# Two layers of multi-query and Hedgehog attention: slab prefetch in the weight fold, and where VectorE closes the query features

## The chip, the cores and the metric

The kernel runs on one core of a Trainium2 chip. The core has TensorE (PE in the profile; PEld are its weight loads), VectorE (DVE), ScalarE (ACT), GpSimd (POOL) and SyncE (SP, which issues most DMAs). Each engine works through its own queue in order and waits on semaphores for the others. The metric is the device time of one execution in microseconds; lower is better.

## The reference

The input is x of 2048 tokens by 576 features in fp32. Four residual blocks follow one another: A, B, A, B, the same weights each time.

```python
# A: softmax attention, 32 query heads of 18, one shared key and value head
q = (x @ wq) per head;  k = x @ wk;  v = x @ wv
o = softmax(q k^T * 18**-0.5) @ v;  return o @ wo
# B: Hedgehog linear attention, 32 heads of 18
q, k, v = x @ wqkv per head
phi_q = concat(softmax(q @ w_phi), softmax(-(q @ w_phi)));  phi_k likewise
kv = phi_k^T v;  z = sum_s phi_k
return (phi_q kv) / (phi_q z + 1e-6) @ wo
x = x + A(layernorm(x)); x = x + B(layernorm(x)); and both once more
```

## The kernel before

**Layers and stages.** One "layer" of the kernel is a block A and a block B. Each layer has an attention stage (softmax attention over 16 token tiles of 128, in two groups of 16 heads each, so 32 groups) and a tail that reads out the linear attention and projects the next layer's queries. The attention stage is the bulk of the time: in the profile 112 to about 1240 us for the first layer and 1478 to about 2565 us for the second.

**A group.** For each of 16 key tiles `expose` (L990) multiplies scores into a two-bank PSUM tile (`sc`, L518; three such tiles exist) and ScalarE takes their exponential (L994). `add_values` (L804) multiplies the exponentials with the values (L806) into one PSUM bank. `burst` puts three such score tiles ("units") on TensorE, then two or three steps of values.

**Two PSUM banks for everything else.** `homes` holds two banks, called `ps` and `acc`. One collects the current group's values. The other is the spare in which all background work is done, one product at a time. When a group opens (`values`, t = 0) the two change places: the spare becomes the new group's bank, so whatever product stands in it must have been copied out by VectorE before the first value product of the group can start, and the old bank is the spare once `finish_group` has transposed it out (L908, into `turned`).

**Background work.** The generator `stream` runs beside the groups. In the first layer it first folds w_phi into the query and key weights (`fold_phi`, ten slabs of 128 rows, loaded by ScalarE's DMA queue, L332). Then it runs `output` for finished tiles (the projection with `wo`, L240 with `on`, and the residual add, L304) and `mix` for 14 of the 16 tiles. A `mix` makes, in this order: two key products, two value products, two query products (14 matmuls each, L240), and the state products (`update_state`, L595) which VectorE adds to `kv` (L601).

**Features.** After each key or query product `feature_start` copies the bank out (L551), takes maxima and minima (L553, L554) and subtracts them (L555, L556); ScalarE takes the exponential (L558). `feature_end`, the "closing", sums, inverts and multiplies (L563, L564, L565). For the queries, whose tile is `featq`, both halves are closed at the end of `mix`. Then VectorE transposes 32x32 blocks of the whole query features into `pht` (L647, in `block_transpose`), and four DMAs spill that to DRAM (L652, `phi<-pht`). The rest of this generator is put into the queue `slow`.

**The next tile's tokens.** `turn_tokens`, called from `update_state` right behind the state sum, splits the next tile's transposed tokens into two parts (`xs`, lines 133, 134, 673, 674). The tokens were transposed earlier by `flip` (L658, L647 on `xc`, also through `pht`), through DRAM; `flip` is called only while `slow` is empty.

**What sets the order.** `tick` takes one step from each of the queues `urgent`, `loads` and `slow`. `in_order` pins TensorE's and VectorE's instructions in the order in which the Python code makes them. ScalarE's, GpSimd's and SyncE's instructions are placed by the framework's scheduler, by readiness as it estimates it.

## Time and profile before

| | us |
|---|---|
| median of 3 runs | 2717.02 (2711.14 to 2718.07) |
| profiled execution | 2717.63 |
| its span, first to last instruction | 2715.9 |
| TensorE busy | 2609.6 (96%) |
| ScalarE busy | 2149.7 (79%) |
| VectorE busy | 1258.2 (46%) |
| mean granted TensorE clock | 0.986 |

The profile is of one execution; times in it count from its first instruction. In a row of the timeline stand the start, the duration, the engine, the line of the kernel, the operation, the output and inputs by tile names, their sizes, and in brackets how long the engine stood idle before it and who ended that. A row of waits gives the total, how often, and the longest. Value products of one step run four at a time on different columns of the array, so that durations of single rows overlap.

### The profile page before, as it was taken

To read this page: it belongs to the slowest core of one execution; us is meant where nothing else is said; L and a number is where in the kernel's file an instruction comes from. 1 tells how busy PE (TensorE), PEld (TensorE's weight loads), DVE (VectorE), ACT (ScalarE), POOL (GpSimd) and SP (SyncE) were. 2 spreads that over 40 slices of the span, in tenths; PEclk is the share of its full clock that TensorE was granted. 3 is DMA by queue.
4 is the path that set the end of the run, shared out by engine and by line. 5 is a ranking of instruction groups with operands and counts; after the bars stand their busy time and mean duration, and the time that the engine had idled before them with its cause. 6 is when DMAs were issued, how large, how long until landed. Compare 5 with 4: busy or idle time off the path is not lost. (4 is left out here: it accounts for less than half of the span.)

```text
span 2715.9 us, 55458 instructions
## 1 busy us (share of the span) xinstructions
PE 2609.6 (96%) x22030; PEld 1454.6 (54%) x22030; DVE 1258.2 (46%) x2867; ACT 2149.7 (79%) x2511; POOL 56.8 (2%) x98
## 2 busy tenths in 40 slices
PE   7989999999999999999998999999999999999989
PEld 6633345554555544456997244444444444444588
DVE  8532244445454444445775124444444444444455
ACT  4588898998889879995334999999999999999711
POOL 1000000000000000001000000000000000000010
PEclk9999999999999999999999999999999999999989
DMA  6554134222223212214755412222222222221164
GB/s 192 169 186 140 50 111 130 69 66 58 53 67 72 59 46 57 57 47 112 233 155 161 144 51 59 59 59 59 59 59 59 59 59 59 57 59 48 40 190 144
DMA packets 476349, 245.05 MB, mean 90 GB/s; under 512 B 222706, under 2 KB 433842, under 8 KB 476082
## 3 DMA queue, kind: packets, MB, share of 16 engines
q1 hardware_dynamic: 474610, 238.46, 31.8%
q8 instruction: 177, 2.90, 0.5%
q10 hardware_dynamic: 1472, 2.95, 0.3%
q14 instruction: 90, 0.74, 0.1%
HBM read 133.86 MB, written 105.51 MB: 88 GB/s over the span
## 5 line engine op out<-in xcount | busy, mean ns | idle before, releaser
L994 ACT ACTIVATE pt<-sc 128x1024 f32<-128x1024 f32 x2036 | 1925.4, 1047 | 211.2 <-PE sc L518 191.1
L518 PE MATMUL sc<-qst,kst 56*128 56x512 f32 x3840 | 687.1, 449 | 23.5 <-ACT pt L994 23.0
L518 PEld LDWEIGHTS sc<-qst,kst 56*128 56x128 f32 x3840 | 317.2, 184 | 534.3 <-ACT pt L994 479.4
L806 PE MATMUL acc<-pt,vst 128*32 128x512 f32 x4096 | 499.0, 600 | 0.6 <-DVE featk L551 0.2
L806 PE MATMUL ps<-pt,vst 128*32 128x512 f32 x4048 | 483.5, 601 | 6.5 <-DVE featk L551 6.1
L806 PEld LDWEIGHTS ps<-pt,vst 128*32 128x32 f32 x4048 | 110.1, 109 | 237.4 <-issue 224.2
L806 PEld LDWEIGHTS acc<-pt,vst 128*32 128x32 f32 x4096 | 106.0, 109 | 218.4 <-issue 212.1
L240 PE MATMUL ps<-wahi,xs 128*128 128x288 f32 x792 | 174.5, 306 | 5.7 <-DVE featk L551 3.4
L304 DVE TENSOR_TENSOR xc<-xc,acc 128x288 f32<-128x288 f32 x60 | 27.2, 453 | 321.1 <-PE acc L240 321.1
L240 PEld LDWEIGHTS ps<-wahi,xs 128*128 128x128 f32 x792 | 131.6, 191 | 14.1 <-DVE featk L551 4.2
L240 PE MATMUL ps<-walo,xs 128*128 128x288 f32 x440 | 130.1, 298 | 0.0
L240 PE MATMUL acc<-wdhi,on 128*128 128x288 f32 x540 | 119.7, 307 | 2.0 <-DMA on<-od 2.0
L240 PE MATMUL ps<-wchi,xs 128*128 128x288 f32 x495 | 111.2, 310 | 0.0
L131 ACT ACTIVATE xs<-ps 128x512 fp32r<-128x512 f32 x36 | 21.4, 595 | 112.6 <-PE ps L290 106.3
L396 PE MATMUL ps<-xsc,wbhi 128*128 128x256 f32 x576 | 107.6, 286 | 0.7 <-ACT xsc L131 0.7
L551 DVE COPY featq<-ps 128x288 f32<-128x288 f32 x47 | 21.5, 458 | 179.7 <-PE ps L240 179.6
L418 ACT ACTIVATE pc<-ps 128x256 fp32r<-128x256 f32 x80 | 30.4, 384 | 93.4 <-PE ps L396 90.4
L240 PEld LDWEIGHTS acc<-wdhi,on 128*128 128x128 f32 x540 | 87.9, 187 | 23.9 <-issue 21.1
L396 PEld LDWEIGHTS ps<-xsc,wbhi 128*128 128x128 f32 x576 | 91.4, 193 | 1.6 <-ACT xsc L131 1.1
L240 PEld LDWEIGHTS ps<-wchi,xs 128*128 128x128 f32 x495 | 82.8, 192 | 16.8 <-issue 15.6
L240 PE MATMUL acc<-wdlo,on 128*128 128x288 f32 x300 | 88.2, 294 | 0.0
L396 PE MATMUL ps<-xsc,wblo 128*128 128x256 f32 x320 | 86.1, 284 | 0.0
(260 smaller groups left out, 3066.6 us busy)
## 6 DMA issues: line engine op xcount, KB each, us to landing
qst<-qd SPq DMA_DIRECT2D x360, 72.0 KB
od<-parts SPq DMA_DIRECT2D x512, 36.0 KB
pht<-phi SPq DMA_DIRECT2D x32, 540.0 KB
qd<-pc SPq DMA_DIRECT2D x64, 256.0 KB
phi<-pht SPq DMA_DIRECT2D x112, 144.0 KB
on<-od SPq DMA_DIRECT2D x60, 256.0 KB
xd<-xc SPq DMA_DIRECT2D x32, 288.0 KB
flipped<-pht SPq DMA_DIRECT2D x112, 72.0 KB
```

The source lines that it names most:

```text
L131: A.activation(dst_hi, src, AF.Copy)
L240: T.matmul(dst, xs[:, slot, :], w[half][:, k, c0 : c0 + HALF], start=(n == 0), stop=(n == last))
L304: V.tensor_add(xr, xr, po)
L396: T.matmul(po, lhs, xsc[:, slot, :], start=(n == 0), stop=(n == LASTP))
L418: A.activation(pc[:, 0, :], po, AF.Copy)
L518: T.matmul(sc, kst[head_rows(h), t * P : (t + 1) * P], q[head_rows(h), h // 2, :], start=True, stop=True)
L551: V.tensor_copy(e[:, hs, 0, :], src)
L806: T.matmul(acc[32 * j : 32 * j + 32, :], vst[:, t, :], pts[j], start=first, stop=last)
L994: A.activation(pt, sc, AF.Exp, scale=SCALE)
```

## The change

Three edits. First, `fold_phi` loads three slabs before its loop, and in the loop asks for slab n + 3 at the end of turn n instead of for slab n + 2 at its start. Second, the closing of the first half of the query features moves from the end of `mix` to the end of `queries`, ahead of the state products; the second half stays where it was. Third, the transposition into `pht` is no longer made at the end of `mix` but in the first step that `tick` takes of the generator in `slow`; the four spills follow four ticks later as before, counted from there.

```diff
-        st, following = fetch(0), fetch(1)
+        slabs_in = deque(fetch(n) for n in range(3))
...
-        short(pl, st)
+        short(pl, slabs_in[0])
         yield -110
         for n, (half, k) in enumerate(units):
-            later = fetch(n + 2)
+            st = slabs_in.popleft()
...
-            short(pl, following)
+            short(pl, slabs_in[0])
+            slabs_in.append(fetch(n + 3))
             nc.sync.dma_start(scratch[half, k * P : (k + 1) * P, :], fo[:, :D])
-            st, following = following, later
...
         if copies is A:
             for b in range(2):
                 feature_end(e, b, G)
+        else:
+            feature_end(e, 0, V)
...
         yield from update_state(ek, vb, st, ps, after=after)
-        for b in range(2):
-            feature_end(eq, b, V)
-        blocks = bw.tile([P, NKG, P], F32, name="pht").rearrange("p a b -> p (a b)")
-        spilling = block_transpose(blocks[:, : 2 * D], eq.rearrange("p h s d -> p (h s d)"), spill[i], SPILL)
-        next(spilling)
-        slow.append(spilling)
+        feature_end(eq, 1, V)
+
+        def spilling():
+            blocks = bw.tile([P, NKG, P], F32, name="pht").rearrange("p a b -> p (a b)")
+            yield from block_transpose(blocks[:, : 2 * D], eq.rearrange("p h s d -> p (h s d)"), spill[i], SPILL)
+
+        slow.append(spilling())
```

The changed kernel's line numbers are 2 higher from L613 on and 3 higher behind `mix`: L647 is L649 there, L908 is L911, L994 is L997.

TensorE's rows are in the same order in both kernels through both attention stages. On VectorE, around the state sum of the first layer's tenth mixer tile (the one at 965 us in the profile), before:

```order
L555 TENSOR_TENSOR featq<-fmin,featq 128x16x18
L556 TENSOR_TENSOR featq<-featq,fmax 128x16x18
L908 STREAM_TRANSPOSE turned<-acc 128x512
L601 TENSOR_TENSOR kv<-kv,ps 128x288
L133 CAST xs<-xn 128x512
```

And with the change:

```order
L556 TENSOR_TENSOR featq<-featq,fmax 128x16x18
L563 TENSOR_REDUCE fz<-featq 128x32
L564 RECIPROCAL fz<-fz 128x32
L565 TENSOR_TENSOR featq<-featq,fz 128x576
L911 STREAM_TRANSPOSE turned<-acc 128x512
L601 TENSOR_TENSOR kv<-kv,ps 128x288
L133 CAST xs<-xn 128x512
```

The three instructions of the first closing stand ahead of the closed group's transposition, the state sum and the token split. A few rows on, the same queue and tile, before:

```order
L134 TENSOR_TENSOR parts<-osb,parts 128x512
L563 TENSOR_REDUCE fz<-featq 128x32
L564 RECIPROCAL fz<-fz 128x32
L565 TENSOR_TENSOR featq<-featq,fz 128x576
L563 TENSOR_REDUCE fz<-featq 128x32
L564 RECIPROCAL fz<-fz 128x32
L565 TENSOR_TENSOR featq<-featq,fz 128x576
L647 STREAM_TRANSPOSE pht<-featq 128x1152
L551 COPY featk<-ps 128x16x18
```

And with the change:

```order
L134 TENSOR_TENSOR parts<-osb,parts 128x512
L563 TENSOR_REDUCE fz<-featq 128x32
L564 RECIPROCAL fz<-fz 128x32
L565 TENSOR_TENSOR featq<-featq,fz 128x576
L551 COPY featk<-ps 128x16x18
L553 TENSOR_REDUCE fmax<-featk 128x16
L554 TENSOR_REDUCE fmin<-featk 128x16
L555 TENSOR_TENSOR featk<-fmin,featk 128x16x18
L556 TENSOR_TENSOR featk<-featk,fmax 128x16x18
L649 STREAM_TRANSPOSE pht<-featq 128x1152
```

One closing is left ahead of the next tile's copy, and the transposition stands behind that copy and its four followers. It does so at seven of the 28 tiles, six of them in the first layer; at the others the transposition stays ahead of the next copy.

On ScalarE, from the query exponentials of the sixth tile (737 us) to the seventh's, before:

```order
L558 ACTIVATE featq<-featq 128x576
L994 ACTIVATE pt<-sc 128x1024 x9
L558 ACTIVATE featk<-featk 128x576
L994 ACTIVATE pt<-sc 128x1024 x2
L558 ACTIVATE featk<-featk 128x576
L994 ACTIVATE pt<-sc 128x1024 x31
```

And with the change:

```order
L558 ACTIVATE featq<-featq 128x576
L997 ACTIVATE pt<-sc 128x1024 x6
L558 ACTIVATE featk<-featk 128x576
L997 ACTIVATE pt<-sc 128x1024 x6
L558 ACTIVATE featk<-featk 128x576
L997 ACTIVATE pt<-sc 128x1024 x30
```

The next tile's first key exponential stands three score tiles further ahead, behind six of them instead of nine. The same holds for the tile at 799 us.

On SyncE, from the first tile's spills (453 us), before `L652 DMA phi x4`, the next group's query loads (L502, L509), then the flipped tokens (L652); with the change three of the spills, the query loads, the fourth spill, then the flipped tokens.

## The prediction

> **What bounds the kernel now.** I read the page's busy times first, then the busy times by stage, then TensorE's own waits in each stage, and last the timeline around its longest stops.

> ```profile
> span 2715.9 us, 55458 instructions
> PE 2609.6 (96%) x22030; PEld 1454.6 (54%) x22030; DVE 1258.2 (46%) x2867; ACT 2149.7 (79%) x2511; POOL 56.8 (2%) x98
> 400.00:1200.00 800.00, 781.84 (x6574) 401.12 (x6574) 385.83 (x780) 711.12 (x771) 7.03 (x13) 1.00 0.27 67
> 1500.00:2500.00 1000.00, 990.14 (x8028) 469.84 (x8024) 409.94 (x824) 925.28 (x1001) 7.56 (x14) 1.00 0.25 62
> ```

> The last two rows are the two attention stages with the mixer's tiles in them (columns: length, then busy PE, PEld, DVE, ACT, POOL, then clock, DMA share, GB/s). TensorE is busy for 781.84 of 800 us in the first layer and 990.14 of 1000 in the second. All that a reordering of VectorE can win there is TensorE's idle time: 18 us and 10 us. Its waits, the first five rows from the first layer (400 to 1200), the last from the second (1500 to 2500), say for whom (total, times, longest):

> ```profile
> PE ps L806 <- DVE featk L551: 6.1, 1, 6.1
> PE sc L518 <- ACT pt L994: 4.3, 11, 1.2
> PE ps L240 <- DVE featk L551: 3.4, 2, 1.7
> PE ps L240 <- DVE turned L908: 1.3, 3, 0.5
> PE acc L240 <- DMA on<-od: 0.6, 1, 0.6
> PE sc L518 <- ACT pt L994: 9.3, 28, 0.7
> ```

> In the second layer nothing but the exponentials is waited for; VectorE holds up nobody, so I look for no gain there. In the first layer one stop of 6.1 us and two of 1.7 end with L551, the copy that empties a PSUM bank. These three are what the change can reach.

> **The first edit (slabs).** The order shows ScalarE's queue beginning with three slab loads in both kernels, and the later ones at the same rows; TensorE's and VectorE's rows are unchanged up to the first mixer tile. The prefetch was already there, so this edit is worth nothing; if the order hid a difference it would touch only the fold stage before 400 us.

> **The second and third edits, at the long stop.** The closing (L563, L564, L565) of the query features' first half now stands ahead of `turned` (L908) and the state sum; L647 stands behind the copy.

> ```profile
> 962.22 2.78 PE L806 MATMUL acc<-pt,vst 128*32 128x512 f32 x24
> 969.03 0.97 PE L518 MATMUL sc<-qst,kst 56*128 56x512 f32 x6
> 976.09 5.05 PE L806 MATMUL ps<-pt,vst 128*32 128x512 f32 x24 [6.09 <-DVE featk L551]
> 965.07 0.72 DVE L908 STREAM_TRANSPOSE turned<-acc 128x512 f32<-128x512 f32 x1 [1.45 <-PE acc L806]
> 970.51 0.75 DVE L563 TENSOR_REDUCE fz<-featq 128x32 f32<-128x576 f32 x1
> 972.36 0.74 DVE L563 TENSOR_REDUCE fz<-featq 128x32 f32<-128x576 f32 x1
> 974.32 1.38 DVE L647 STREAM_TRANSPOSE pht<-featq 128x1152 f32<-128x1152 f32 x1
> 975.62 0.42 DVE L551 COPY featk<-ps 128x288 f32<-128x288 f32 x1
> ```

> One closing takes 972.36 - 970.51 = 1.85 us, or 974.32 - 972.36 = 1.96 to the next instruction; L647 delays the copy by 975.62 - 974.32 = 1.30. The closing put ahead of L908 finds 1.45 us of idle time there, so L908 and all behind it, TensorE's next product too, come 1.85 - 1.45 = 0.40 late. The second closing starts at 970.91, the copy at 970.91 + 1.96 = 972.87, and TensorE goes on 0.47 later, as now (975.62 to 976.09): 973.34 instead of 976.09, **2.75 us won**. TensorE then stands idle from 969.03 + 0.97 + 0.40 = 970.40 for 2.94 us.

> The stop has a second price: 24 value products took 5.05 us behind it, and 2.78 at 962. The clock explains the 2.27 us between (columns as above; the clock is the third number from the end):

> ```profile
> 975.00:980.00 5.00, 3.91 (x20) 0.99 (x24) 2.77 (x6) 0.68 (x1) 0.00 (x0) 0.50 0.56 138
> 301.04 0.30 PE L337 MATMUL ps<-idf,fstage 128*72 128x128 f32 x1 [1.80 <-DVE featk L362]
> 301.00:303.00 2.00, 1.96 (x9) 0.27 (x9) 0.29 (x1) 0.35 (x1) 0.00 (x0) 0.61 0.34 82
> 303.00:305.00 2.00, 2.00 (x13) 1.24 (x10) 0.00 (x0) 1.09 (x2) 0.00 (x0) 0.53 0.59 190
> ```

> An idle time of 1.80 us at 301 was enough for a halved clock: (0.39 + 0.47) x 2 / 0.5 = 3.4 us of it, which cost 1.7. So I take it that 2.94 us idle still halves the clock, for 1.7 us of loss: 2.27 - 1.70 = **0.57 won**. The ends are 0 and 2.27. Rival D below is the other case.

> [...]

> **The two stops of 1.7 us** (tiles at 737 and 799, alike):

> ```profile
> 737.00 0.46 DVE L601 TENSOR_TENSOR kv<-kv,ps 128x288 f32<-128x288 f32 x1 [1.98 <-PE ps L595]
> 741.06 0.74 DVE L563 TENSOR_REDUCE fz<-featq 128x32 f32<-128x576 f32 x1
> 746.16 0.42 DVE L551 COPY featk<-ps 128x288 f32<-128x288 f32 x1
> 746.64 0.40 PE L240 MATMUL ps<-wahi,xs 128*128 128x288 f32 x1 [1.68 <-DVE featk L551]
> 748.69 0.96 PE L518 MATMUL sc<-qst,kst 56*128 56x512 f32 x6
> 744.59 2.85 ACT L994 ACTIVATE pt<-sc 128x1024 f32<-128x1024 f32 x3 [0.75 <-PE sc L518]
> 748.45 0.69 ACT L558 ACTIVATE featk<-featk 128x576 f32<-128x576 f32 x1 [1.01 <-DVE featk L556]
> 808.24 0.41 PE L240 MATMUL ps<-wahi,xs 128*128 128x288 f32 x1 [1.69 <-DVE featk L551]
> ```

> Here the moved closing fits into the 1.98 us that VectorE idles ahead of L601, so nothing is late. The copy starts at 741.06 + 1.96 = 743.02 instead of 746.16, and TensorE does not stop for it. But the order also moves the key features' exponential (L558) up by three score tiles. It follows the copy by 748.45 - 746.16 = 2.29, so it runs from 745.31 to 746.00, in front of the three score exponentials that now start at 744.59. They then end at 746.0 + 2.85 = 748.85 at the latest, and the last of the next three score pairs (a third of 0.96) cannot be written before: scores end at about 749.1 instead of 749.65. Of 1.68 us, **0.55 is won at each, 1.10 together**; the ends are 0 and 1.7 each.

> **Two places where it costs.** Where `turned` follows at once and TensorE waits for what is behind it:

> ```profile
> 505.40 0.72 DVE L908 STREAM_TRANSPOSE turned<-ps 128x512 f32<-128x512 f32 x1 [0.59 <-PE ps L806]
> 506.04 0.41 DVE L601 TENSOR_TENSOR kv<-kv,acc 128x288 f32<-128x288 f32 x1
> 506.75 1.92 PE L806 MATMUL acc<-pt,vst 128*32 128x512 f32 x16
> 508.61 1.26 PE L518 MATMUL sc<-qst,kst 56*128 56x512 f32 x6
> 610.36 0.72 DVE L908 STREAM_TRANSPOSE turned<-acc 128x512 f32<-128x512 f32 x1 [0.59 <-PE acc L806]
> 611.13 0.77 PE L595 MATMUL acc<-featk,vb 128*32 128x36 f32 x64
> 625.82 0.49 PE L518 MATMUL sc<-qst,kst 56*128 56x512 f32 x2 [1.22 <-ACT pt L994]
> ```

> VectorE idles only 0.59 us there, so the closing makes L908 1.85 - 0.59 = 1.26 late. At 506 the state sum L601 moves to 507.30, and with the same 0.47 the values into `acc` start at 507.77 instead of 506.75, 1.02 late; the scores behind them took 1.26 instead of 0.97, waiting for ScalarE, and give back 0.29: **0.73 lost**. At 610 the state products L595 write the bank that L908 empties, so they are 1.26 late; some comes back at the 1.22 us stop at 625.82, which has the exponential in front of it that now moves three tiles up. **I take 0.70 lost**, ends 0 and 1.26.

> The other tiles have the 1.96 us slot as at 737, or no product that needs the bank soon: nothing. The four spills that follow each L647 leave at most about 2 us later (a copy and its group, 2.29, less what was won), and on SyncE's in-order queue the loads behind them go later with them: head outputs (`on`) and the next group's queries (`qst`), which TensorE did not wait for by more than the 0.6 us that its list of waits shows for `on`. I put them at nothing; their upper end is rival C.

> **Sum:** -2.75 - 0.57 - 1.10 + 0.73 + 0.70 = -3.0 us. The profiled execution took 2717.63 us, so 2714.6; it lies 0.6 above the median of the three runs (2717.02), and on the median's footing the forecast is **2714.0**.

> **Rivals.** *D, the clock stays whole:* the idle time shrinks from 6.09 to 2.94 us, less than one halved stretch of 3.4 us, and if only an idle time as long as such a stretch halves the clock, all of the 2.27 comes back: 2712.3. For it: the stops of 1.68 and 1.69 us left no slow products behind them; against it: the 1.80 us at 301. *A, faster:* the late copies were the only trouble, ScalarE and the two places of 0.59 us absorb the rest, and the clock stays whole: 2.75 + 2.27 + 1.68 + 1.69 = 8.4 won, 2708.6. For it: ScalarE is busy only 711 of 800 us. Against it: the 1.80 us at 301, and TensorE has no slack to absorb anything. [...] *C, slower:* a spill held up on SyncE's queue stops VectorE.

> ```profile
> SPq L502 <- PE sc L518: 167.4, 18, 23.1
> 693.19 0.78 DVE L647 STREAM_TRANSPOSE pht<-xc 128x576 f32<-128x576 f32 x1 [3.00 <-DMA phi<-pht]
> ```

> For the tile at 453 the fourth spill now stands behind the next group's query loads, and those waited for TensorE 18 times for 167.4 us, 9.3 on average. The next tile's transposition (L647 on `xc`) reuses `pht` and waits for that spill; once, at 693, it stood 3.00 us. If VectorE gets there before the spill is read, the copies behind it are late and TensorE stops: with an average hold, 2717.0 + 9.3 = 2726.3. It decides where the transposition comes earlier than about 3 us after the fourth spill's issue. Against it: the order also moves that transposition one value product later (past L582 and a closing), and at 693 TensorE did not stop.

> **How the numbers follow.** A measurement of this kernel tells about 0.3% (8.1 us) from no change. Chances: forecast 0.50, D 0.14, A 0.13, B 0.13, C 0.10. The range reaches from 2707.0 (A, with a median that moves by part of the 5.9 us by which the fastest run of before lies below it) to 2720.0 (B and the highest run, 2718.07); C is left out. Faster by over 0.3% is A and the lower tails of the forecast and of D (0.07), 0.20; slower is C, 0.10; within it 0.70.

> **What would show it.** Right: the wait of L806 for L551 near 970 is about 2.9 us, the two of 1.7 for L551 are gone with new waits of about 1 us for L994 in their place, L595 near 611 waits 1.3 us for `turned`, and the second layer is unchanged. Wrong: a wait of DVE L647 for `phi` above 3 us (C), no halved clock near 975 (D or A), or a fold stage that is shorter.

## The result, and the profile after

The changed kernel took 2711.91 us (median of 20 runs, 2704.79 to 2718.26), the kernel before 2717.08 in the runs beside it (20 runs, 2711.14 to 2719.74). The ratio is 0.9984, with a 95% interval of 0.9977 to 0.9991: 4.3 us faster, between 2.4 and 6.2 (the medians lie 5.2 apart; the ratio is not their quotient). The forecast was 3.0 us faster, which lies in this interval; the timing alone does not tell 3.0 from 4.3. The profiled execution took 2713.51 us.

The page's span and first row, and the two attention stages from the busy times by stage:

```profile
span 2711.7 us, 55457 instructions
PE 2607.3 (96%) x22030; PEld 1451.1 (54%) x22030; DVE 1258.2 (46%) x2867; ACT 2149.2 (79%) x2511; POOL 56.8 (2%) x98
400.00:1200.00 800.00, 785.50 (x6594) 402.28 (x6593) 384.18 (x779) 712.47 (x774) 7.03 (x13) 1.00 0.27 67
1500.00:2500.00 1000.00, 989.78 (x8024) 469.56 (x8026) 415.89 (x834) 925.96 (x1003) 7.56 (x14) 1.00 0.24 61
```

VectorE and ScalarE do the same work. TensorE idles 14.5 of the 800 us instead of 18.2, and in the second layer 10.2 instead of 9.9. Its waits in the first layer:

```profile
PE sc L518 <- ACT pt L997: 5.2, 15, 0.7
PE ps L809 <- DVE featk L551: 3.1, 2, 2.9
PE acc L595 <- DVE turned L911: 1.1, 1, 1.1
PE acc L809 <- DVE kv L601: 0.9, 1, 0.9
PE ps L240 <- DVE xs L133: 0.4, 1, 0.4
```

The 6.1 us stop is now 2.9, the two of 1.7 are gone from the list, ScalarE is waited for 15 times instead of 11, and the last three rows are new. The prediction named all of these: the last row is the 0.40 us by which it had TensorE's next product late ahead of the long stop. Where the time came from is seen by the start of the same TensorE product in both traces:

| start before, us | start after, us | later by | the place since the row above |
|---|---|---|---|
| 493.71 | 493.46 | -0.25 | fold stage and first tiles |
| 512.55 | 513.24 | +0.69 | the values that wait for the state sum, 506 |
| 626.25 | 627.53 | +1.28 | the state products that wait for `turned`, 611 |
| 737.94 | 739.44 | +1.50 | |
| 753.23 | 754.23 | +1.00 | first stop of 1.7 us |
| 799.53 | 800.58 | +1.05 | |
| 814.80 | 815.37 | +0.57 | second stop of 1.7 us |
| 906.43 | 907.19 | +0.76 | |
| 913.85 | 914.07 | +0.23 | a wait of 0.58 us for `on`, gone |
| 981.97 | 978.57 | -3.39 | the long stop and its slow clock |
| 1307.42 | 1303.59 | -3.83 | transition to the second layer |
| 2590.05 | 2586.00 | -4.05 | second layer |

Between 494 and 982 us the change gains 3.39 - 0.25 = 3.14 us; the forecast's sum was 3.0.

### The profile page after: what moved, and what is told of

Its sections match the earlier page's. It is cut to its first block, busy times and chain, and to the rows that moved or that the text cites. A ratio compares the mean times of both kernels' runs of the same rounds, so it can differ in the third digit from the quotient of the medians.

```text
span 2711.7 us, 55457 instructions
## 1 busy us (share of the span) xinstructions
PE 2607.3 (96%) x22030; PEld 1451.1 (54%) x22030; DVE 1258.2 (46%) x2867; ACT 2149.2 (79%) x2511; POOL 56.8 (2%) x98
## 5 line engine op out<-in xcount | busy, mean ns | idle before, releaser
L997 ACT ACTIVATE pt<-sc 128x1024 f32<-128x1024 f32 x2036 | 1925.3, 1047 | 211.6 <-PE sc L518 191.3
L518 PE MATMUL sc<-qst,kst 56*128 56x512 f32 x3840 | 688.6, 449 | 24.5 <-ACT pt L997 24.0
L518 PEld LDWEIGHTS sc<-qst,kst 56*128 56x128 f32 x3840 | 317.5, 184 | 536.0 <-ACT pt L997 483.7
L240 PE MATMUL ps<-wahi,xs 128*128 128x288 f32 x792 | 174.0, 306 | 2.6 <-ACT xs L131 0.6
L240 PEld LDWEIGHTS ps<-wahi,xs 128*128 128x128 f32 x792 | 131.2, 190 | 10.9 <-PE sc L518 3.3
L240 PE MATMUL ps<-walo,xs 128*128 128x288 f32 x440 | 129.9, 298 | 0.0
L240 PE MATMUL acc<-wdhi,on 128*128 128x288 f32 x540 | 119.8, 307 | 1.4 <-DMA on<-od 1.3
L240 PE MATMUL ps<-wchi,xs 128*128 128x288 f32 x495 | 110.2, 308 | 0.0
L551 DVE COPY featq<-ps 128x288 f32<-128x288 f32 x47 | 21.5, 458 | 179.7 <-PE ps L240 179.6
L240 PEld LDWEIGHTS acc<-wdhi,on 128*128 128x128 f32 x540 | 87.9, 187 | 23.5 <-issue 21.1
L240 PEld LDWEIGHTS ps<-wchi,xs 128*128 128x128 f32 x495 | 81.9, 190 | 16.8 <-issue 15.6
L240 PE MATMUL acc<-wdlo,on 128*128 128x288 f32 x300 | 88.2, 294 | 0.0
```

The source lines that it names most:

```text
L240: T.matmul(dst, xs[:, slot, :], w[half][:, k, c0 : c0 + HALF], start=(n == 0), stop=(n == last))
L518: T.matmul(sc, kst[head_rows(h), t * P : (t + 1) * P], q[head_rows(h), h // 2, :], start=True, stop=True)
L551: V.tensor_copy(e[:, hs, 0, :], src)
L997: A.activation(pt, sc, AF.Exp, scale=SCALE)
```

## The experiments

Each was timed beside the kernel before: the slabs alone and the run with the spill held back beside 2716.25 us (23 runs), the others beside 2715.78 (18 runs). A difference in us that "the time" gives is the ratio's, times that median; it can differ from the difference of the medians. "Net" below is the same difference of starts as in the table, over 494 to 982 us of one profiled execution; outside this stage the starts of different executions wander by several us (at 494, from 0.65 early to 3.86 late).

**The second edit alone.** The closing is moved; the transposition stays at the end of `mix`, the slabs as before.

```diff
+        else:
+            feature_end(e, 0, V)
 ...
-        for b in range(2):
-            feature_end(eq, b, V)
+        feature_end(eq, 1, V)
```

> Only the second edit: the first closing moves ahead of the state products, the transposition stays at the end of the mixer tile, ahead of the next copy. Theory of the forecast: the copy at the long stop comes 1.85 - 0.40 = 1.45 us earlier, so TensorE stands 6.09 - 1.85 = 4.2 us near 970 and the clock still halves; at 745 and 807 the stops for L551 go, but ScalarE's wait for the key features takes their place, 0.15 won at each; the closing costs the same two new waits as in the change, about 0.9 us near 507 (values for the state sum) and 1.15 near 612 (state products for turned). Sum 0.4 to 1.0 us faster than before: ratio 0.9996 to 0.9999, not to be told from 1. Rival 'the late copies were all': 4 us or more faster.

Measured: 2725.93 us (5 runs), ratio 1.0046, interval 1.0032 to 1.0060. It is slower, and the expectation missed. SyncE's issues in its timeline (start, duration, what is transferred), first in the kernel before, then here:

```profile
544.67 0.36 SPq L88 DMA_DIRECT2D xc<-in_A_x_dram  x1
545.52 0.39 SPq L843 DMA_DIRECT2D on<-od  x1
559.76 2.34 SPq L652 DMA_DIRECT2D phi<-pht  x4
```

```profile
546.76 0.36 SPq L88 DMA_DIRECT2D xc<-in_A_x_dram  x1
560.02 0.31 SPq L654 DMA_DIRECT2D phi<-pht  x1
560.44 0.51 SPq L844 DMA_DIRECT2D on<-od  x1
SPq L654 <- DVE pht L649: 21.5, 3, 12.8
563.65 0.58 PE L240 MATMUL acc<-wdhi,on 128*128 128x288 f32 x1 [8.15 <-DMA on<-od]
560.00:565.00 5.00, 0.88 (x3) 0.57 (x3) 0.00 (x0) 0.00 (x0) 0.00 (x0) 0.50 0.73 171
```

The first three rows here are SyncE's issues again, the fourth its wait from the list of waits, the fifth TensorE's row, the last the clock (third number from the end). No instruction for SyncE was edited. But the scheduler placed one spill of the second mixed tile ahead of the loads of `on` instead of behind them. SyncE waited 12.8 us for the transposition (L649) before that spill, and the loads placed behind it left 13.7 us after the transfer of `xc` instead of 0.85. TensorE's projection stood still for 8.15 us, and the clock was halved around its restart (0.50 from 560 to 565 us). By starts, the kernel lost 0.93 us at 506 and 12.9 us in all by 626. Another 1.66 us were lost between 738 and 753, behind a second halved stretch at 763.8 in this trace, to which the last section comes back; net over the stage: +13.6.

**The same, with that spill held back.** This is the test of that reading.

```diff
+        st["nth"] = st.get("nth", 0) + 1
-        spilling = block_transpose(..., spill[i], SPILL)
+        spilling = block_transpose(..., spill[i], SPILL + (4 if st["nth"] == 2 else 0))
```

> The second edit alone, as in the run that came out at 1.0046, but with the spill of the second mixed tile held back four ticks more, so that on SyncE's queue the four loads of `on` stand ahead of it again, as in the kernel before. TensorE's and ScalarE's orders are those of the run at 1.0046; on VectorE one tile's flip comes a few instructions later. Theory (the loss of that run was the spill that stood ahead of the loads of `on`, not the closing): the stop of 8.15 us at 555 us and the halved clock behind it are gone, TensorE waits for `on` less than 1 us there, ratio 0.9994 to 1.000. Rival (an early closing with the transposition in the same turn costs by itself): ratio 1.003 or more, with the wait at another line of the same stage.

Measured: 2715.86 us (12 runs), ratio 1.0004, interval 0.9994 to 1.0014. SyncE's rows and TensorE's remaining long stop:

```profile
550.27 0.39 SPq L845 DMA_DIRECT2D on<-od  x1
559.61 2.33 SPq L654 DMA_DIRECT2D phi<-pht  x4
976.64 1.93 PE L808 MATMUL ps<-pt,vst 128*32 128x512 f32 x8 [4.25 <-DVE featk L551]
```

With the loads in front again the stop at 555 is gone, and so is the loss (1.95 us by 626 where it was 12.9): the place of the spill was its cause, not VectorE's time for the closing. The early closing alone is worth nothing that can be told (the time says 1.1 us slower, with an interval of -1.6 to +3.8). It shortens the long stop from 6.09 to 4.25 us, the size of one closing, but pays 0.93 at 506 and 1.02 by 626, and the two stops of 1.7 us come back in full as waits for ScalarE (net 0.0 at each). Net over the stage: -1.3.

**The third edit alone.** Both closings at the end of `mix`, the transposition in the spilling turn.

```diff
-        spilling = block_transpose(...)
-        next(spilling)
-        slow.append(spilling)
+        def spilling(): ... yield from block_transpose(...)
+        slow.append(spilling())
```

> Only the third edit: both closings stay at the end of the mixer tile, the transposition moves into the turn of the spills. Theory of the forecast: the copy at the long stop comes 1.30 us earlier, TensorE stands 4.8 us near 970, the clock still halves; at 745 and 807 the stops for L551 shrink from 1.7 to 0.4 and ScalarE's wait takes 0.8 of the rest, 0.45 won at each; no wait near 507 and 612, since no closing moves. Sum 2.2 us faster than before (ratio 0.9992), more than the second edit alone. Rival 'the early closing is what pays': about 0 for this one.

Measured: 2714.94 us (11 runs), ratio 0.9996, interval 0.9987 to 1.0005. TensorE's row at the long stop, and its wait for the copies in the other places:

```profile
976.09 1.94 PE L808 MATMUL ps<-pt,vst 128*32 128x512 f32 x8 [4.69 <-DVE featk L551]
PE ps L240 <- DVE featk L551: 0.6, 2, 0.3
```

The stop is 1.40 us shorter, the transposition's length (1.38). In this trace the two stops of 1.7 us give 0.47 and 0.46 net: nearly all that the changed kernel won at these places (0.50 and 0.48) needs only this edit. Nothing is paid at 506 and 611, and the net is -3.6, while the time gave -1.1 us with an interval of -3.5 to +1.4. So what this edit wins alone rests on one trace. The idle times at 970 do add up: 1.40 and 1.84 shorter alone, 3.24 together.

**The first edit alone.** Only the slabs requested ahead.

> Only the first edit: three slabs to fold requested ahead, the closings and the transposition as before. The order on TensorE, VectorE and ScalarE is that of before. Forecast's step (the slabs are worth nothing): ratio 1.000, within 0.001, and TensorE's products up to 280 us stand within 0.7 us of before's. Rival (the 0.5 us that the changed kernel was ahead at 204 us came from the slabs): products after 204 us earlier by 0.5 us, ratio 0.9998; if slabs queued early held up other loads, 1.001 or more.

Measured: 2716.49 us (12 runs), ratio 1.0000, interval 0.9989 to 1.0012. Net over the stage: 0.0. Its products at 204 us start 0.48 us early, but those of the three kernels above, which have no slab edit, start 0.68 to 1.15 early. The 0.54 at that place in the changed kernel is a difference of the size that executions show there anyway, and the slab edit is worth nothing that can be told (the time's interval is -3.0 to +3.3 us).

**The closing between the two query products.** The change, with the first half closed ahead of the second half's product. It should take away the two losses.

```diff
+            if b and copies is V:
+                feature_end(e, 0, V)
 ...
-        else:
-            feature_end(e, 0, V)
```

> The change, with the first closing written between the two query products, where VectorE idles, and not behind them. Theory of the forecast: the two new waits near 507 (0.9 us) and 612 (1.15 us) and the 0.4 us near 966 are gone; the stop near 970 stays at 2.9 us with one halved stretch of 3.4 us. Sum 1.5 to 2 us faster than the change, 4.4 to 5 us faster than before: ratio to before 0.9982 to 0.9984 by the profile, shifts read at the same products. Rival 'TensorE wins back such delays by itself' : the waits go but the time stays that of the change.

Measured: 2711.25 us (8 runs), ratio 0.9983, interval 0.9972 to 0.9995. TensorE's first waits, its row at the long stop, and the clock there (the third number from the end) in two stretches:

```profile
PE sc L518 <- ACT pt L997: 5.2, 15, 0.8
PE ps L809 <- DVE featk L551: 3.1, 2, 2.9
PE ps L240 <- DVE turned L911: 1.3, 3, 0.5
975.26 1.07 PE L809 MATMUL ps<-pt,vst 128*32 128x512 f32 x8 [2.86 <-DVE featk L551]
970.40:973.81 3.41, 2.00 (x15) 1.35 (x13) 3.27 (x6) 2.75 (x4) 0.00 (x0) 1.00 0.05 12
973.81:977.23 3.42, 1.97 (x20) 0.68 (x24) 3.28 (x8) 1.24 (x3) 0.00 (x0) 1.00 0.31 74
```

The waits for the state sum and for `turned` at the state products are gone. By starts, nothing is lost at 506, and 0.47 is won by 626 where the change lost 1.53 between 494 and 626. The clock stayed whole (1.00) behind a stop of 2.86 us, where the expectation had a halved stretch. This is taken up at the end. It adds to the net, which is -6.7 in this execution; the time says -4.6, with an interval of -7.6 to -1.4. Against the changed kernel's 0.9984 the ratios do not tell the expected 2 us.

**Also the second half closed in the spilling turn.** Then, at the seven tiles where the turn comes behind the next copy, no closing is left between the group's end and that copy.

```diff
-        feature_end(eq, 1, V)
         def spilling():
+            feature_end(eq, 1, V)
             blocks = ...
```

> As the kernel with the first closing between the query products, and the second closing goes with the transposition into the turn of the spills, behind the next copy. Theory of the forecast: the copy at the long stop follows the group's split at once (970.5), TensorE stands about 1.0 us there and the clock stays whole: 5.1 + 2.3 us won; the copies at 745 and 807 come 1.96 us earlier still, so ScalarE's exponential of the key features finds them ready and all of 1.68 and 1.69 is won; no new waits. Sum about 10.7 us faster than before, ratio 0.996, and about 6 us faster than the change. Rival 'ScalarE's wait remains': 7.5 us faster than before. Rival 'an idle time of 1 us still halves the clock': 9 us.

Measured: 2705.22 us (5 runs), ratio 0.9956, interval 0.9942 to 0.9969, faster than both kernels. TensorE's first waits, then its row at the long stop, VectorE's copy ahead of it, and the clock:

```profile
PE sc L518 <- ACT pt L996: 3.4, 11, 0.4
PE ps L240 <- DVE turned L910: 1.3, 3, 0.5
PE ps L808 <- DVE featk L551: 1.2, 2, 1.0
971.39 2.78 PE L808 MATMUL ps<-pt,vst 128*32 128x512 f32 x24 [1.01 <-DVE featk L551]
970.88 0.45 DVE L551 COPY featk<-ps 128x288 f32<-128x288 f32 x1
970.00:975.00 5.00, 3.99 (x34) 1.16 (x30) 4.79 (x10) 3.83 (x5) 0.00 (x0) 1.00 0.26 61
```

The copy starts 4.74 us before the kernel before's (975.62), or 5.1 counted from the rows ahead of it, which stand 0.38 later in this trace. The 24 value products take 2.78 us at once, at a clock of 1.00. Each stop of 1.7 us is now won in full, 1.72 and 1.69 net. Net over the stage: -10.8; the time says -11.9, with an interval of -15.8 to -8.4 (the medians differ by 10.6). The expectation was 10.7.

## Why the prediction was right, step by step

**The long stop.** Right. VectorE's rows, TensorE's row and the stretches of the clock in the changed kernel:

```profile
965.62 0.71 DVE L911 STREAM_TRANSPOSE turned<-acc 128x512 f32<-128x512 f32 x1
971.05 0.74 DVE L563 TENSOR_REDUCE fz<-featq 128x32 f32<-128x576 f32 x1
972.90 0.45 DVE L551 COPY featk<-ps 128x288 f32<-128x288 f32 x1
975.10 1.37 DVE L649 STREAM_TRANSPOSE pht<-featq 128x1152 f32<-128x1152 f32 x1
973.40 4.34 PE L809 MATMUL ps<-pt,vst 128*32 128x512 f32 x24 [2.85 <-DVE featk L551]
969.77:973.18 3.41, 0.78 (x6) 0.29 (x4) 3.27 (x7) 2.85 (x3) 0.00 (x0) 1.00 0.20 49
973.18:976.60 3.42, 3.20 (x16) 0.79 (x20) 3.18 (x6) 0.68 (x1) 0.00 (x0) 0.50 0.16 38
```

The copy starts at 972.90 (forecast 972.87), TensorE at 973.40 (973.34), after 2.85 us idle (2.94). That the starts agree so closely is luck: the rows ahead stand 0.23 us later in this trace, which the forecast could not know, and two small terms made up for it. The closing made `turned` 0.32 late where the forecast had 0.40, and the copy followed 1.85 behind the closing's start where it had 1.96. The clock is halved for 3.4 us, and the 24 products take 4.34 instead of 5.05: 0.71 won where 0.57 stood. That it was halved at all was likely, not certain: with the closing between the query products it stayed at 1.00 behind a stop of 2.86 us (last section). The whole gain here is 3.62 against 3.32. Between 815 and 982 it is 3.96, because the wait of 0.58 us for `on` at 907, which the forecast left standing, is gone (0.53 won) and 0.19 was lost on the way there. Why that wait went is not shown; with the slabs alone it was 0.4 long, with the closing between the query products there were three, 1.2 in all.

**The two stops of 1.7 us.** Right in kind and nearly in size: 0.50 and 0.48, against 0.55 each. The rest did come back as waits for ScalarE, behind the key exponential that runs earlier:

```profile
744.40 0.45 DVE L551 COPY featk<-ps 128x288 f32<-128x288 f32 x1
746.72 0.69 ACT L558 ACTIVATE featk<-featk 128x576 f32<-128x576 f32 x1 [1.39 <-DVE featk L556]
749.28 0.51 PE L518 MATMUL sc<-qst,kst 56*128 56x512 f32 x2 [0.24 <-ACT pt L997]
750.20 0.50 PE L518 MATMUL sc<-qst,kst 56*128 56x512 f32 x2 [0.41 <-ACT pt L997]
```

The exponential starts 2.32 after the copy (forecast 2.29), and ScalarE stands idle for 1.39 us ahead of it. The prediction put both edits into the copy's earlier start and spoke of the moved closing; the runs give the gain to the moved transposition, since it won 0.47 and 0.46 alone and the closing alone won nothing here. With the copy another closing earlier, as in the last experiment, the stop is won whole.

**The two losses.** Right in place. TensorE's rows:

```profile
507.44 1.93 PE L809 MATMUL acc<-pt,vst 128*32 128x512 f32 x16 [0.87 <-DVE kv L601]
612.90 0.77 PE L595 MATMUL acc<-featk,vb 128*32 128x36 f32 x64 [1.15 <-DVE turned L911]
624.35 0.50 PE L518 MATMUL sc<-qst,kst 56*128 56x512 f32 x2 [0.74 <-ACT pt L997]
```

At 506 the values came 0.94 late (forecast 1.02), and the 0.29 that the scores behind them were to give back is not found in the next product, which is 0.94 late too: 0.73 was too little. At 611 the state products came 1.08 later than the 0.69 they had before that place, and the stop at 625, now 0.74 instead of 1.22, gave back 0.49: 0.59 where 0.70 stood.

**The steps at nothing.** The slabs are at nothing, and so is the second layer: its starts drift from -3.83 to -4.05. The execution is 0.25 us early before 494 and gains another 0.66 behind 982. Runs without the slab edit are 0.85 to 2.64 late at 494, and with the slabs alone the starts move by +1.56 and then -1.94 behind 982, so neither is told from a difference between executions.

**The sum.** The net of 3.14 lies nearer to the forecast's 3.0 than its terms do. The `on` wait (0.53) and 0.30 more at the long stop came on top; against them stand 0.12 less at the two stops, 0.10 more at the two losses, and 0.46 lost in small pieces at 626 to 738, 753 to 800 and 815 to 906, which the forecast had at nothing. That these nearly cancel is luck.

**The rivals.** A (8.4 us won) did not come, and neither did B, no gain: the time lies 2.4 to 6.2 us below before's. D (a whole clock) did not come in this execution (0.50 behind 2.85 us), but the closing between the query products shows that it can (1.00 behind 2.86 us). C did not come in the changed kernel; but its first half, a spill held up on SyncE's queue, is real (12.8 us). It appeared where the prediction had seen only 0.6 us to be waited for: a spill ahead of the loads of `on`, with the second edit alone. It did not stop VectorE, as C had it, but TensorE, for 8.15 us. With the third edit put in beside the second, the spills stand behind these loads (558.76 us; the first load at 546.11).

## What to carry to other kernels

When a copy that frees a bank ends a stop, move everything off its way that can follow it: each piece moved here shortened the stop by its own length (1.40 for the transposition, 1.84 for a closing), and with the last one the clock stayed whole (1.00) in its trace. Put a moved step where the engine idles for as long as the step takes: here a closing of 1.85 us put into 1.98 us of idle time (737 us) added no wait ahead of the copy, put into 1.45 (965) it made what follows 0.32 us late, and put into 0.59 (506 and 611) it made TensorE 0.94 and 1.08 us late. Where a scheduler places the DMAs, read the queue's order again after every edit on another engine: one spill of 0.31 us ahead of four loads cost about 11 us in the trace (12.9 less 1.95 by 626).

## What the hardware showed beyond that

```profile
298.09:301.50 3.41, 1.61 (x13) 0.86 (x15) 2.88 (x7) 3.07 (x4) 0.00 (x0) 0.99 0.05 13
301.50:304.91 3.41, 3.41 (x16) 1.15 (x9) 0.17 (x1) 1.00 (x2) 0.00 (x0) 0.51 0.49 143
```

That cell was busy for 1.61 us, and the clock of the next is 0.51. Over all cells of the eight traces that ran at the full clock (the first 20 us left out), sorted by the share in which TensorE was idle:

| idle share of a cell | cells | next one halved |
|---|---|---|
| below 25% | 5934 | 0 |
| 25 to 47% | 99 | 7 |
| 47 to 53% | 34 | 31 |
| above 53% | 62 | 61 |

So in these traces the change comes near half a cell, 1.6 to 1.8 us of idle time (47 to 53%), but it is no sharp limit. Seven cells that were idle for only 28 to 44% were followed by a halved one too. One of them stands in this stage, with the closing alone: TensorE stopped for ScalarE for 0.84 and 0.41 us near 762, was busy for 2.15 us of that cell, and the 24 value products behind it took 4.46 us instead of 2.78. What else counts is not shown. Behind the stop of 1.01 us in the last experiment the clock was whole (1.00). Behind the stop of 2.85 us it was halved (0.50); behind the one of 2.86, cut by the grid near its middle, it was not (1.00). The prediction assumed a halved clock behind 2.94 us; by these rows that was likely, not certain. This is read from the traces, since no run set the phase.
